# Router logits with three token blocks in each column group: shifted gate weights, two transposes, one copy and one bias product a batch

## The chip, the cores and the metric

One core of a Trainium2 chip runs the kernel. The metric is the device time of one execution in microseconds (us). Three runs of the kernel before gave 432.74, 435.83 and 438.20 us, so the median is 435.83 us.

## The reference

Two stages are computed, all in float32. The first is a chunked attention: 4 batches, 8 heads, 768 positions of width 64; a chunk of 32 queries sees 8 memory keys and a window of up to 56 keys around itself. Its output, as 3072 tokens of width 512, goes through a top-1 mixture of 8 experts. The change is in the router, the first lines of the second stage:

```python
logits = x @ w_gate + modality_bias[modality_id]      # (3072, 512) @ (512, 8)
e_idx = np.argmax(logits, axis=1)
probs = softmax(logits)
gate_w = probs[np.arange(N), e_idx]
for e in range(E):                                    # 8 experts, F = 1024
    h = np.maximum(x[mask] @ w1[e], 0.0)
    out[mask] = gate_w[mask, None] * (h @ w2[e])
```

## The kernel before

The order of the instructions is written out by hand for every engine (TensorE, VectorE, ScalarE, GpSimd, SyncE); an engine works through its own list in order.

**Attention.** There are 16 units `u`, two heads each, and each is done in two halves `hf`; the loop at L970 goes over the 32 halves `i` (and two more to drain). In a half TensorE makes scores (L328, 24 records: 12 products, each run twice for float32), transposes the scores (L345), makes the averages (L357) and transposes the result (L382); every second half it also transposes the next keys (L310, L314) or queries (L292). ScalarE takes most of it out of PSUM (L320, L297, L347, L385), VectorE subtracts the maximum and normalises (L336, L339, L365 to L370), GpSimd completes the windows of values (`share_v`, L271) and stores x (L375), SyncE issues the loads. Four PSUM banks named `tr` are handed out in turn by `bank()`.

**The routing of a batch.** Four units make one batch of 768 tokens, six blocks of 128. `xTs[u]` holds x transposed, with 128 features of unit u on the partitions and 768 tokens along the row, in one of five places of `xall`; the sixth place of `xall` is the buffer `lgs`. `route(b)` (L529) is a generator. First it makes the logits: for each half of the tokens, four products (L534), one for each unit g, write to the four column groups of one bank: 32 rows for each group, of which 8 are the experts' and 24 come from zero weights in `wg`. ScalarE copies each bank (384 columns) to `lgs` (L537). Later six transposes (L543), one for each block of 128 tokens, put tokens on the partitions, into two banks; two products (L526, `own_bias`) add the bias of each token's modality beside them; and two sums on VectorE (L548) add the four groups and the bias into `l`. Then come the maximum, the exponential, the ranks (L575 to L580) and the table of tokens by expert (L683).

**How the routing is woven in.** Each `yield "v"` ends a short VectorE step, each `yield "full"` waits for a place in TensorE's list. For batches 0 to 2 `pump` (L393) takes these steps out one by one at fixed places of the loop; the logits of batches 0, 1 and 2 go out at i = 10, 18 and 25 (the call `pump(1, ("tiled",))`, L1071), their transposes at i = 11, 19 and 26. Batch 3 is routed by `further` (L1132) between the first products of the experts.

**Experts.** The rest is matrix products of gathered tokens with float32 weights split into two parts (L844, L825, L828, L856), with VectorE and ScalarE making the parts (L755, L756). At the hand-over from attention to experts GpSimd gathers tokens (L765) and SyncE loads the first expert's weights (L748, L752).

GpSimd also makes the constants of the bias: `bias_rows` (L238 to L243) at i = 8. `small_loads` (L170) loads the gate weights at i = 1, and L928 zeroes `wg` at the start.

Of the kernel before, what the change touches and what calls it, by code (L numbers as in the profile page):

```python
# [9 lines left out]
F32 = mybir.dt.float32  # L10
# [7 lines left out]
AX = mybir.AxisListType  # L18
# [3 lines left out]
P = 128  # L22
B, H, S, D = 4, 8, 768, 64
NMEM = 8
NCH = S // 32
NT = S // P
E, DM, DF = 8, 512, 1024
# [18 lines left out]
def tile_chunk_attention_top1_moe(  # L46
# [14 lines left out]
    nc = tc.nc  # L61
# [4 lines left out]
    const = ctx.enter_context(tc.tile_pool(name="const", bufs=1))  # L66
    dram = ctx.enter_context(tc.tile_pool(name="dram", bufs=1, space=DRAM))
    ps = ctx.enter_context(tc.tile_pool(name="ps", bufs=2, space=PSUM))
    rt = ctx.enter_context(tc.tile_pool(name="rt", bufs=1))
# [5 lines left out]
    ld = c_ld.enter_context(tc.tile_pool(name="ld", bufs=3))  # L75
# [8 lines left out]
    def bank():  # L84
        return ps.tile([P, 512], F32, name="tr", tag="tr", bufs=4)
# [37 lines left out]
    ident = const.tile([P, P], F32, name="ident")  # L123
# [15 lines left out]
        nc.gpsimd.memset(mvx[g][:, :, D:D + 1], 1.0)  # L139
    edge_v(2)  # L140

    wg = const.tile([P, 4, 32], F32, name="wg")
    mod_i = ld.tile([N // P, P, 2], I32, name="mod_i", bufs=1)
    bias_b = ld.tile([N // P, 2, E], F32, name="bias_b", bufs=1)
    mods = const.tile([N // P + 1, P], F32, name="mods")
    rows_b = const.tile([N // P + 1, N // P, E], F32, name="rows_b")
# [21 lines left out]
                nc.vector.tensor_copy(vws[i][r, h, c, D:D + 1], vmask[r, m:m + 1])  # L168

    def small_loads():  # L170
        nc.sync.dma_start(wg[:, :, 0:E], w_gate.rearrange("(c p) e -> p c e", p=P))
        nc.sync.dma_start(mod_i.rearrange("t p w -> t (p w)"), modality.bitcast(I32).rearrange("(t x) -> t x", t=N // P))
        nc.sync.dma_start(bias_b, m_bias.rearrange("m e -> (m e)").partition_broadcast(N // P).rearrange("p (m e) -> p m e", e=E))
        nc.sync.dma_start(rows_b[N // P:], bass.AP(tensor=m_bias.tensor, offset=0, ap=[[0, 1], [0, N // P], [1, E]]))
# [28 lines left out]
    def more_constants():  # L203
        nc.vector.tensor_copy(iota5[:, :, 0:26], iota_i[:, 0:130].rearrange("p (a b) -> p a b", a=5))
        yield
        nc.vector.tensor_copy(iota3[:, :, 0:64], iota_i.rearrange("p (a b) -> p a b", a=3))
        yield
        nc.vector.tensor_scalar(rev[:, 0], iota3[:, 0, 0:E], -1.0, float(E), op0=ALU.mult, op1=ALU.add)
        yield
        nc.vector.memset(ones_b, 1.0)  # L210
        yield
        nc.vector.tensor_scalar(tri_b.rearrange("p (a b) -> p a b", a=2), iota3[:, 0:2, 0:64], pcol, None, op0=ALU.is_gt)
        yield

        nc.vector.tensor_scalar(tokn, iota3[:, 0, 0:N // P], float(P), pcol, op0=ALU.mult, op1=ALU.add)
        yield
        nc.vector.tensor_scalar(tokn, tokn, -EMPTY, None, op0=ALU.add)
        yield
        nc.vector.tensor_scalar(tokm, tokn, -1.0, None, op0=ALU.mult)
        yield  # L220
        nc.vector.memset(table, EMPTY)
        yield
        nc.vector.tensor_copy(tab_i[:, E * HI:NCOL], table[:, E * HI:NCOL])
        yield
        nc.vector.tensor_scalar(tail_row, pcol[0:64], 31.5, None, op0=ALU.is_gt)
        yield
        nc.vector.tensor_scalar(col0, iota3[0:64, 0, 0:E], float(HI), -float(E * HI), op0=ALU.mult, op1=ALU.add)
        yield
        nc.vector.memset(tot, 0.0)
        yield  # L230
        nc.vector.tensor_copy(four.rearrange("p (g t) -> p g t", g=4), ident[:, 0:REST].unsqueeze(1).to_broadcast([P, 4, REST]))
        yield
        nc.vector.tensor_scalar(quarter, pcol, 31.5, None, op0=ALU.is_gt)
        yield
        for r in (63.5, 95.5):
            nc.vector.scalar_tensor_tensor(quarter, pcol, r, quarter, op0=ALU.is_gt, op1=ALU.add)

    def bias_rows():  # L238
        nc.gpsimd.memset(mods, 1.0)
        nc.gpsimd.tensor_copy(mods[0:N // P], mod_i[:, :, 0])  # L240
        nc.gpsimd.tensor_sub(bias_b[:, 1:2], bias_b[:, 1:2], bias_b[:, 0:1])
        own = ident[0:N // P, 0:N // P].unsqueeze(2).to_broadcast([N // P, N // P, E])
        nc.gpsimd.tensor_mul(rows_b[0:N // P], bias_b[:, 1:2].to_broadcast([N // P, N // P, E]), own)  # L243


    qrs, qTs, xTs, xbs, PTs, kts, qts, scs, sbs, avs = ({} for _ in range(10))
# [130 lines left out]
    def trans_x(u, hf):  # L377
        xb = xbs[u]
        t = bank()
        warm(t, {(NU - 2, 0): 3, (NU - 2, 1): 2, (NU - 1, 0): 2}.get((u, hf), 0))  # L380
        for i in range(3):
            nc.tensor.transpose(t[:, i * P:(i + 1) * P], xb[:, 3 * hf + i, :], ident)  # L382
        if hf == 0:
            xTs[u] = xall[:, u % 5]
        nc.scalar.copy(xTs[u][:, 384 * hf:384 * hf + 384], t[:, 0:384])  # L385
        if hf == 1 and not NU - 3 <= u < NU - 1:
            store_x(u)


    xall = rt.tile([P, 6, S], F32, name="xall")  # L390
    routing, now = [], [0]

    def pump(k, pe=(), late=False):  # L393
# [128 lines left out]

    G = P + 32

    def own_bias(lt, T):
        nc.tensor.matmul(lt[:, 0:3 * G].rearrange("p (t c) -> p t c", c=G)[:, :, P:P + E], mods, rows_b[:, T:T + 3, :],  # L526
                         start=True, stop=True)

    def route(b):  # L529
        lgs = xall[:, 5]  # L530
        for hf in range(2):
            lg = bank()
            for g in range(4):
                nc.tensor.matmul(  # L534
                    lg[32 * g:32 * g + 32, 0:384], wg[:, g, :], xTs[4 * b + g][:, 384 * hf:384 * hf + 384], start=True, stop=True
                )
            nc.scalar.copy(lgs[:, 384 * hf:384 * hf + 384], lg[:, 0:384])  # L537
        yield "full"
        sh = [P, NT, E]
        l = sm.tile(sh, F32, name="l")  # L540
        lts = [bank() for _ in range(2)]
        for t in range(NT):
            nc.tensor.transpose(lts[t // 3][:, t % 3 * G:t % 3 * G + P], lgs[:, t * P:(t + 1) * P], ident)  # L543
        for i, lt in zip((0, 3), lts):
            own_bias(lt, b * NT + i)
        for i, lt in zip((0, 3), lts):
            parts = lt[:, 0:3 * G].rearrange("p (t g e) -> p t e g", t=3, g=5)[:, :, 0:E, :]
            nc.vector.reduce_sum(l[:, i:i + 3].unsqueeze(3), parts, axis=AX.X)  # L548
            yield "v"
        mx = sm.tile([P, NT, 1], F32, name="rmx")  # L550
        nc.vector.reduce_max(mx, l, axis=AX.X)
        yield "v"
# [95 lines left out]
        for t in range(NT):  # L648
# [8 lines left out]
            T = b * NT + t  # L657
# [267 lines left out]

    masks()
    nc.gpsimd.iota(iota_i, [[1, 192]], base=0, channel_multiplier=0)
    nc.gpsimd.memset(wg, 0.0)  # L928
    blank_v(0, 3)
    load_v(0)  # L930
    load_qk(1)
# [2 lines left out]
    t = ps.tile([P, 512], F32, name="av", tag="av", bufs=2)  # L934
# [28 lines left out]
    t = ps.tile([P, 512], F32, name="sc", tag="sc", bufs=2)  # L963
# [5 lines left out]
    n = len(units)  # L969
    for i in range(n + 2):  # L970
        live = i < n
        u, hf = units[i] if live else (NU, i % 2)
# [89 lines left out]
        for _ in range(4 if i > 2 else 0):  # L1062
            next(constants, None)
        if i == 8:
            bias_rows()
        if i == 5:
            nc.scalar.copy(mvx[1][:, :, 0:D], mvn[:, 1:2].to_broadcast([P, NCH, D]))
# [107 lines left out]

    tails = plan_tails()

    w1m = xall.rearrange("p a b -> p (a b)")[:, 0:4 * DF].rearrange("p (c f) -> p c f", c=4)

    def slot(s):  # L1180
        ahead = s != NSURE - 1
# [150 lines left out]
```

## Time and profile before

| | us |
|---|---|
| three runs, median | 435.83 (432.74 to 438.20) |
| the profiled execution | 436.68 |
| its span | 434.83 |
| outside the span | 1.85 |
| TensorE busy | 413.4 (95% of the span) |
| VectorE, ScalarE, GpSimd busy | 334.6, 299.4, 236.9 |

An engine's busy time is the union of its records; a product's end is modelled, so a busy TensorE need not be at its peak. The view by stretches tells how busy each engine is in one stage, the chain of waits tells which work ended last there, and the groups by line give the duration of one instruction.

### The profile page before, as it was taken

What the parts mean: (1) busy time and instruction counts of PE and PEld (TensorE: products, weight loads), DVE (VectorE), ACT (ScalarE), POOL (GpSimd) and SP (SyncE); (2) the same over time, 40 slices, a digit from 0 to 9 for tenths busy, and PEclk for the clock granted to TensorE, in tenths of its full rate; (3) what the DMA queues carried; (4) which work ended last, traced back from release to release, by engine and by line L of the source; (5) the groups of instructions that cost most, each with busy time, mean ns of one, the idle gap of its engine ahead of it and who ended that gap; (6) DMA issues with size and microseconds to landing.
All of it is one profiled execution on the core that took longest, in us unless ns stands there. A gap on an engine that the chain in (4) does not pass through costs nothing.

```text
span 434.8 us, 11397 instructions
## 1 busy us (share of the span) xinstructions
PE 413.4 (95%) x3867; PEld 343.5 (79%) x3870; DVE 334.6 (77%) x800; ACT 299.4 (69%) x597; POOL 236.9 (54%) x320
## 2 busy tenths in 40 slices
PE   7988999999996999999999999999999999999994
PEld 4776787778864878989898887888888788888882
DVE  6888589687774878957988888767988787978750
ACT  7776778687743564755767677767888786878750
POOL 8947768768583233877655564355577055620101
PEclk9999999999998999999999999999999999999998
DMA  9879999999759220117414629988977424220101
GB/s 220 177 196 223 253 255 202 252 226 227 150 145 328 97 51 0 52 49 148 97 50 98 233 90 274 236 269 237 293 270 239 102 54 100 69 79 2 49 3 54
DMA packets 82543, 66.81 MB, mean 154 GB/s; under 512 B 50659, under 2 KB 71339, under 8 KB 82476
## 3 DMA queue, kind: packets, MB, share of 16 engines
q1 hardware_dynamic: 75276, 46.36, 44.3%
q0 software_dynamic: 6784, 19.50, 14.3%
q8 instruction: 33, 0.54, 0.6%
q14 instruction: 34, 0.28, 0.2%
q10 hardware_dynamic: 416, 0.13, 0.1%
HBM read 84.64 MB, written 12.76 MB: 224 GB/s over the span
## 4 chain that ended last, share of the span: by engine, by line
PE 57%; issue 15%; DMA 10%; POOL 5%; DVE 5%; ACT 3%; another core or an unknown queue 1%; SPq 1%; POOLq 1%; ACTq 0%; DVEq 0%
PE tr L844 11%; PE sc L856 10%; PE av L856 9%; PE tr L825 7%; PE tr L828 4%; PE av L357 3%; DMA vw<-in_v_dram 3%; DMA out_dram<-o,ix_now 3%; DMA q<-in_q_dram 3%; PE sc L328 2%; ACT kbd L320 2%; POOL xg L765 2%; PE tr L382 2%; PE tr L345 2%; PE tr L310 1%
## 5 line engine op out<-in xcount | busy, mean ns | idle before, releaser
L756 DVE TENSOR_TENSOR w<-raw,w 128x512 fp32r<-128x512 f32 x96 | 67.3, 744 | 4.1 <-ACT w L755 3.2
L825 PE MATMUL tr<-xt,w 128*128 128x512 f32 x256 | 70.1, 395 | 0.0
L856 PE MATMUL av<-wh,h 128*128 128x512 f32 x192 | 62.7, 398 | 0.6 <-ACT wh L755 0.6
L271 POOL COPY vw<-vw 24x1472 f32<-24x1472 f32 x32 | 45.6, 1425 | 22.8 <-DMA vw<-in_v_dram 21.6
L755 ACT CAST w<-raw 128x512 fp32r<-128x512 f32 x96 | 53.8, 620 | 1.5 <-DMA raw<-in_moe_w_dram 1.5
L856 PE MATMUL sc<-wh,h 128*128 128x512 f32 x160 | 51.7, 397 | 0.0
L825 PEld LDWEIGHTS tr<-xt,w 128*128 128x128 f32 x256 | 44.3, 189 | 7.3 <-DVE h L838 0.4
L844 PE MATMUL tr<-xt,w 128*128 128x256 f32 x384 | 48.1, 284 | 0.7 <-DVE xt L820 0.7
L844 PEld LDWEIGHTS tr<-xt,w 128*128 128x128 f32 x384 | 46.8, 191 | 2.2 <-DVE xt L820 0.9
L320 ACT COPY kbd<-tr 64x672 f32<-64x672 f32 x57 | 44.5, 781 | 4.3 <-PE tr L314 2.8
L828 PEld LDWEIGHTS tr<-xt,w 128*128 128x128 f32 x256 | 39.3, 189 | 5.5
L856 PEld LDWEIGHTS av<-wh,h 128*128 128x128 f32 x192 | 36.1, 188 | 9.3 <-ACT wh L755 1.0
L861 POOL DMA_INDIRECT out_dram<-o,ix_now x22 | 25.8, 1173 | 29.9 <-ACT o L860 24.6
L828 PE MATMUL tr<-xt,w 128*128 128x256 f32 x256 | 40.7, 281 | 0.0
L834 DVE TENSOR_TENSOR hs<-tr,hs 128x256 f32<-128x256 f32 x64 | 26.8, 418 | 17.0 <-ACT hs L831 16.0
L856 PE MATMUL av<-wl,h 128*128 128x512 f32 x96 | 38.2, 397 | 0.4 <-DVE wl L756 0.2
L347 ACT ACTIVATE PT<-tr 128x384 f32<-128x384 f32 x32 | 15.8, 494 | 30.2 <-PE tr L345 24.6
L835 ACT ACTIVATE h<-hs 128x256 fp32r<-128x256 f32 x64 | 26.8, 419 | 13.9 <-DVE hs L834 12.6
L856 PEld LDWEIGHTS sc<-wh,h 128*128 128x128 f32 x160 | 30.1, 188 | 7.1 <-issue 0.2
L837 DVE TENSOR_TENSOR wl<-vw,wh 128x512 fp32r<-128x512 f32 x48 | 33.2, 692 | 2.1
L838 DVE SCALAR_TENSOR_TENSOR h<-hs,h 128x256 fp32r<-128x256 f32 x64 | 27.8, 434 | 7.8 <-ACT h L835 7.3
L831 ACT COPY hs<-tr 128x256 f32<-128x256 f32 x64 | 23.5, 368 | 13.8 <-PE tr L828 11.2
(265 smaller groups left out, 919.5 us busy)
## 6 DMA issues: line engine op xcount, KB each, us to landing
raw<-in_moe_w_dram SPq DMA_DIRECT2D x96, 256.0 KB
vw<-in_moe_w_dram SPq DMA_DIRECT2D x72, 256.0 KB
k<-in_k_dram SPq DMA_DIRECT2D x16, 384.0 KB
q<-in_q_dram SPq DMA_DIRECT2D x16, 384.0 KB
xd<-xb POOLq DMA_DIRECT2D x16, 384.0 KB
kbd<-in_moe_w_dram SPq DMA_DIRECT2D x24, 256.0 KB
vw<-in_v_dram SPq DMA_DIRECT2D x32, 184.0 KB
xall<-in_moe_w_dram SPq DMA_DIRECT2D x4, 1024.0 KB
```

Of the source, the lines that this page charges most:

```text
L271: nc.gpsimd.tensor_copy(vw[r0:r0 + 24, h, 1:NCH, 0:D], vw[r0 + 32:r0 + 56, h, 0:NCH - 1, 0:D])
L320: copy(dst.rearrange("p c (i j) -> p c i j", j=2)[:, :, :, j], win)
L755: nc.scalar.copy(wh[i], raw[i])
L756: (eng or nc.vector).tensor_sub(wl[i], raw[i], wh[i].bitcast(F32))
L825: nc.tensor.matmul(ph, wh[f][:, c * P:(c + 1) * P], xt[:, c].rearrange("p a n -> p (a n)"), start=(c == 0), stop=False, skip_group_check=True)
L828: nc.tensor.matmul(ph[:, 0:256], wl[f][:, c * P:(c + 1) * P], xth[:, c], start=False, stop=(c == 3), skip_group_check=True)
L834: nc.vector.tensor_add(hs, ph[:, 0:256], hs)
L835: nc.scalar.activation(hh[:, f], hs, AF.Relu)
L837: nc.vector.tensor_sub(wl[w], raw[w], wh[w].bitcast(F32))
L838: nc.vector.scalar_tensor_tensor(hl[:, f], hs, 0.0, hh[:, f].bitcast(F32), op0=ALU.max, op1=ALU.subtract)
L844: nc.tensor.matmul(ph, w[f][:, c * P:(c + 1) * P], x[:, c, :], start=(n == 0), stop=(n == 11))
L856: nc.tensor.matmul(pos[t], x, w[8 + f], start=(f == 0 and n == 0), stop=(f == 7 and n == 2))
```

## The change

The zeroed weights now come in three shifted copies. `wg3` has 120 columns for each unit: the 8 weights at columns 0, 40 and 80. A slice of 32 columns from 32k on thus has the weights in its columns 8k to 8k+7. The logits of a batch become twelve products of 256 columns into one bank: for k = 0, 1, 2 and each unit, the tokens of blocks k and 3+k (two runs of 128 columns) are multiplied with slice k and added up, so that the 32 rows of a column group hold three blocks of 8 logits. One copy of 256 columns, two transposes, one bias product of 48 columns and one sum over 48 results of five terms follow. One `yield "v"` falls away. GpSimd builds `wg3` at i = 8 (`gate_weights`), ahead of `bias_rows`; the zeroing of `wg` at the start falls away; `lgs` shrinks from 768 to 256 columns. The load of the gate weights stays where it was and now fills `wg` without gaps.

```diff
-    wg = const.tile([P, 4, 32], F32, name="wg")
+    wg = ld.tile([P, 4, E], F32, name="wg", bufs=1)
+    wg3 = const.tile([P, 4, 3 * 40], F32, name="wg3")
...
-        nc.sync.dma_start(wg[:, :, 0:E], w_gate.rearrange("(c p) e -> p c e", p=P))
+        nc.sync.dma_start(wg, w_gate.rearrange("(c p) e -> p c e", p=P))
...
+    def gate_weights():
+        nc.gpsimd.memset(wg3, 0.0)
+        nc.gpsimd.tensor_copy(wg3.rearrange("p c (q x) -> p c q x", x=40)[:, :, :, 0:E], wg.unsqueeze(2).to_broadcast([P, 4, 3, E]))
...
     def route(b):
-        lgs = xall[:, 5]
-        for hf in range(2):
-            lg = bank()
+        lgs = xall[:, 5 * S:5 * S + 2 * P]
+        lg = bank()
+        for k in range(3):
             for g in range(4):
                 nc.tensor.matmul(
-                    lg[32 * g:32 * g + 32, 0:384], wg[:, g, :], xTs[4 * b + g][:, 384 * hf:384 * hf + 384], start=True, stop=True
+                    lg[32 * g:32 * g + 32, 0:2 * P].rearrange("p (j n) -> p j n", j=2), wg3[:, g, 32 * k:32 * k + 32],
+                    xTs[4 * b + g].rearrange("p (j k n) -> p j k n", j=2, k=3)[:, :, k], start=(k == 0), stop=(k == 2),
+                    skip_group_check=True,
                 )
-            nc.scalar.copy(lgs[:, 384 * hf:384 * hf + 384], lg[:, 0:384])
+        nc.scalar.copy(lgs, lg[:, 0:2 * P])
         yield "full"
...
-        lts = [bank() for _ in range(2)]
-        for t in range(NT):
-            nc.tensor.transpose(lts[t // 3][:, t % 3 * G:t % 3 * G + P], lgs[:, t * P:(t + 1) * P], ident)
-        for i, lt in zip((0, 3), lts):
-            own_bias(lt, b * NT + i)
-        for i, lt in zip((0, 3), lts):
-            parts = lt[:, 0:3 * G].rearrange("p (t g e) -> p t e g", t=3, g=5)[:, :, 0:E, :]
-            nc.vector.reduce_sum(l[:, i:i + 3].unsqueeze(3), parts, axis=AX.X)
-            yield "v"
+        lt = bank()[:, 0:2 * G].rearrange("p (j c) -> p j c", j=2)
+        for j in range(2):
+            nc.tensor.transpose(lt[:, j, 0:P], lgs[:, j * P:(j + 1) * P], ident)
+        nc.tensor.matmul(lt[:, :, P:P + 3 * E], mods, rows_b[:, b * NT:(b + 1) * NT].rearrange("t (j k) e -> t j (k e)", j=2),
+                         start=True, stop=True)
+        parts = lt.rearrange("p j (g x) -> p j x g", x=32)[:, :, 0:3 * E, :]
+        nc.vector.reduce_sum(l.rearrange("p (j k) e -> p j (k e)", j=2).unsqueeze(3), parts, axis=AX.X)
+        yield "v"
...
-    nc.gpsimd.memset(wg, 0.0)
...
         if i == 8:
+            gate_weights()
             bias_rows()
```

## Rows read from the trace of the kernel before

**Rows 1.** The page's first part: busy time of each engine (share of span).

```profile
PE 413.4 (95%) x3867; PEld 343.5 (79%) x3870; DVE 334.6 (77%) x800; ACT 299.4 (69%) x597; POOL 236.9 (54%) x320
```

**Rows 2.** By stretches: from:to, length, busy PE PEld DVE ACT POOL, clock, DMA, GB/s.

```profile
40.00:70.00 30.00, 29.16 (x531) 23.39 (x529) 22.33 (x68) 23.38 (x43) 23.54 (x30) 1.00 1.02 235
70.00:112.00 42.00, 40.97 (x713) 33.84 (x715) 32.36 (x98) 31.29 (x58) 29.46 (x35) 1.00 1.03 236
112.00:140.00 28.00, 22.54 (x369) 16.81 (x363) 17.12 (x54) 14.77 (x30) 18.10 (x36) 0.94 0.69 196
140.00:195.00 55.00, 53.31 (x356) 46.05 (x352) 44.04 (x129) 31.57 (x67) 26.80 (x36) 1.00 0.19 58
195.00:425.00 230.00, 230.00 (x1367) 194.82 (x1366) 186.35 (x371) 169.34 (x359) 108.51 (x131) 1.00 0.52 141
```

**Rows 3.** Chain of waits around batch 0's routing: start, length, what.

```profile
57.13 3.43 DMA vw<-mvx
60.58 0.87 PE av L357 x24
```

**Rows 4.** Timeline of TensorE, batches 0 and 1: start, length, engine, line.

```profile
48.29 1.47 PE L534 MATMUL tr<-xall,wg 128*32 128x384 f32 x16
...
84.09 0.87 PE L357 MATMUL av<-vw,PT 128*32 128x130 f32 x24
...
84.78 0.84 PE L328 MATMUL sc<-kbd,qT 128*32 128x128 f32 x24
```

**Rows 5.** Chain of waits: batches 1, 2 and 3, and L903.

```profile
79.55 1.29 PE tr L534 x16
...
82.95 0.66 PE tr L543 x6
83.61 0.55 PE tr L526 x4
...
109.05 0.66 PE tr L543 x6
...
110.07 0.52 DVE l L548 x2
...
144.94 1.43 PE tr L534 x16
...
267.02 1.86 PE tr L903 x32
```

**Rows 6.** Groups by line and form, ScalarE, VectorE: busy us, mean ns | idle before.

```profile
L831 ACT COPY hs<-tr 128x256 f32<-128x256 f32 x64 | 23.5, 368 | 13.8 <-PE tr L828 11.2
L537 ACT COPY xall<-tr 128x384 f32<-128x384 f32 x8 | 3.7, 486 | 1.5 <-PE tr L534 1.5
L336 DVE TENSOR_REDUCE mx<-sc 128x6 f32<-128x384 f32 x32 | 17.4, 545 | 3.4 <-PE sc L328 3.4
L548 DVE TENSOR_REDUCE l<-tr 128x24 f32<-128x120 f32 x8 | 2.1, 278 | 3.1 <-PE tr L526 3.1
```

**Rows 7.** Timeline of ScalarE at batch 2's logits.

```profile
107.32 0.48 ACT L537 COPY xall<-tr 128x384 f32<-128x384 f32 x1 [1.17 <-PE tr L534]
...
107.99 0.48 ACT L537 COPY xall<-tr 128x384 f32<-128x384 f32 x1 [0.19 <-PE tr L534]
...
109.15 0.49 ACT L347 ACTIVATE PT<-tr 128x384 f32<-128x384 f32 x1 [0.68 <-PE tr L345]
```

**Rows 8.** Groups by line and form, GpSimd.

```profile
L302 POOL COPY kbd<-memT 64x192 f32<-64x192 f32 x28 | 9.7, 347 | 5.1 <-PE sc L328 3.7
L127 POOL MEMSET vw<- 128x256 f32 x3 | 0.9, 314 | 0.0
L928 POOL MEMSET wg<- 128x128 f32 x1 | 0.2, 204 | 0.0
```

**Rows 9.** Timeline of GpSimd behind the bias constants.

```profile
46.95 1.40 POOL L271 COPY vw<-vw 24x1472 f32<-24x1472 f32 x1 [0.74 <-DMA vw<-in_v_dram]
```

**Rows 10.** Chain of waits at the hand-over to the experts.

```profile
127.74 5.48 another core or an unknown queue
```

More of the change, by code (lines that the diff above doesn't have):

```diff
@@ L383, in trans_x @@
         if hf == 0:
-            xTs[u] = xall[:, u % 5]
+            xTs[u] = xall[:, u % 5 * S:(u % 5 + 1) * S]
         nc.scalar.copy(xTs[u][:, 384 * hf:384 * hf + 384], t[:, 0:384])
@@ L387, in trans_x @@
             store_x(u)
-    xall = rt.tile([P, 6, S], F32, name="xall")
+    xall = rt.tile([P, 5 * S + 2 * P], F32, name="xall")
     routing, now = [], [0]
@@ L523, in tile_chunk_attention_top1_moe @@
     G = P + 32
-    def own_bias(lt, T):
-        nc.tensor.matmul(lt[:, 0:3 * G].rearrange("p (t c) -> p t c", c=G)[:, :, P:P + E], mods, rows_b[:, T:T + 3, :],
-                         start=True, stop=True)
     def route(b):
-        lgs = xall[:, 5]
-        for hf in range(2):
-            lg = bank()
+        lgs = xall[:, 5 * S:5 * S + 2 * P]
+        lg = bank()
+        for k in range(3):
             for g in range(4):
                 nc.tensor.matmul(
-                    lg[32 * g:32 * g + 32, 0:384], wg[:, g, :], xTs[4 * b + g][:, 384 * hf:384 * hf + 384], start=True, stop=True
+                    lg[32 * g:32 * g + 32, 0:2 * P].rearrange("p (j n) -> p j n", j=2), wg3[:, g, 32 * k:32 * k + 32],
+                    xTs[4 * b + g].rearrange("p (j k n) -> p j k n", j=2, k=3)[:, :, k], start=(k == 0), stop=(k == 2),
+                    skip_group_check=True,
                 )
-            nc.scalar.copy(lgs[:, 384 * hf:384 * hf + 384], lg[:, 0:384])
+        nc.scalar.copy(lgs, lg[:, 0:2 * P])
         yield "full"
@@ L1176, in tile_chunk_attention_top1_moe @@
     tails = plan_tails()
-    w1m = xall.rearrange("p a b -> p (a b)")[:, 0:4 * DF].rearrange("p (c f) -> p c f", c=4)
+    w1m = xall[:, 0:4 * DF].rearrange("p (c f) -> p c f", c=4)
     def slot(s):
```

## The prediction

> **What bounds the kernel now.** I read the page's busy times first: TensorE is busy for 413.4 of 434.8 us and no other engine comes near [rows 1]. Then the stretches [rows 2], since a share over the whole says little about one place. TensorE is busy for 97 to 98% of the time from 40 to 112 us, where the first three batches are routed, and for 97% from 140 to 195, where the fourth is; from 195 to 425 it never stops. Only from 112 to 140, the hand-over to the experts, does it idle: 5.5 us of 28, and it is the only one of these stretches in which the granted clock is below full (0.94: for part of it at the lower level, 1.2 GHz). One thing disturbs this picture: from 40 to 112 the DMA share is 1.02 to 1.03, so the transfers are as full as TensorE. Hence the third view, the chain of waits: which of the two ended last where the routing stands?
>
> For batch 0 it is the transfers. The chain runs through the transfer of the memory rows until 60.56, and the averages (L357) start at 60.58 [rows 3]; batch 0's logits start at 48.29 [rows 4], and the chain does not pass through them. For batches 1, 2 and 3 it runs through the router's products themselves [rows 5]. So a shorter routing on TensorE should shorten the kernel there, one for one.
>
> **The change part by part, for one batch.**
>
> *Logits.* Eight products of 384 columns become twelve of 256, which is 3072 columns either way. Four column groups run together, so the 16 records of before are four sets in 1.29 us, 0.32 us each [rows 5]. L903 has the same form with 256 columns: 32 records, eight sets, 1.86 us, so 0.23 us a set and 1.40 us for six. That is the upper end, +0.11 us, since L903's piece also carries its way into and out of full-width products. The lower end is the same rate by column: 0. What each product reads comes in two runs of 128 columns now. L357 already reads two runs (of 65), and it starts 0.69 us ahead of L328, six sets of 130 columns [rows 4]: 0.115 us a set and 0.88 ns a column, against 1.29 us / (4 x 384) = 0.84 ns for one run. So two runs cost hardly anything. I take +0.05.
>
> *Transposes.* Six take 0.66 us, 0.11 each [rows 5]; four go: -0.44.
>
> *Bias.* Four records take 0.55 us, 0.14 each [rows 5]. A transpose makes 128 columns in 0.11 us, so 24 columns are about 0.02 us: the price is by record, not by column. Two records of 48 columns then take 0.275 us: -0.275. If the price went by column, nothing would be saved; that is the other end.
>
> TensorE so gets 0.44 + 0.275 - 0.05 = 0.66 us a batch, between 0.33 (bias unchanged, logits +0.11) and 0.72.
>
> *Copy.* Two copies of 384 columns at 486 ns become one of 256; L831 has that form at 368 ns [rows 6]. ScalarE gains 2 x 0.486 - 0.368 = 0.60 us of work a batch. I count it at nothing: TensorE's transposes and averages cover it, and the chain of batches 1 and 3 does not pass through these copies. Without that cover it would be a gain.
>
> The one thing that could speak against it is that one bank now has to be complete before any copy starts. At batch 2 the two copies start at 107.32 and 107.99, and the second ends at 108.47 [rows 7]. The new one starts with the second's start and ends at 107.99 + 0.37 = 108.36, so it is ready sooner; ScalarE waits some 0.67 us longer ahead of it, and its next work, the exponential at 109.15, waited 0.68 us for TensorE anyway. The Trainium skill (Perfetto Trace Analysis, section Matmuls) says to let independent groups go through different banks, so that emptying one overlaps the next one's products, and that larger products are the more efficient. By the first rule the lost overlap could cost up to 0.67 us a batch and bring the sum back to no change; by the rows it is covered, the smaller copy makes up for it, and the sum stays as below. It is a rival.
>
> *Sum on VectorE.* 120 elements take 278 ns, 384 take 545 [rows 6]: 1.01 ns an element, so 240 take 0.40 us, and 0.16 us of 0.56 is saved. It counts only at batch 2, where the chain leaves TensorE into these sums (0.52 us from 110.07 [rows 5]): -0.12.
>
> *Steps.* One `yield "v"` less moves every later VectorE step of batches 0 and 1 one place up in the lists; followed through the loop, the rank products (i = 13 and 21) and the table products (i = 16 and 24) stay where they are. The exponential of the logits moves ahead of the key copies on ScalarE; its input is made one half `i` earlier, so nothing queued behind it waits for more than its own short run, which ScalarE spends anyway. Price: nothing. A batch also takes two `tr` banks fewer, so a product waits for an older bank than before, never for a newer one.
>
> *GpSimd.* Zeroing 128 columns takes 204 ns, 256 take 314 [rows 8]: 0.86 ns a column, so 480 take 0.51 us. The copy writes 96 elements a partition; a copy of 192 takes 347 ns [rows 8], an upper end. Together 0.7 to 0.86 us, ahead of `share_v` at 46.95, which waited 0.74 us for its load [rows 9]. So it is covered, up to 0.12 us late; were the cover gone, `share_v` and the averages that need it would come 0.86 us later. The 204 ns zeroing at the start goes: a gain of at most 0.20 us, counted as nothing.
>
> **The sum.** Batch 0: 0, since the transfers end last there (other end -0.66). Batch 1: -0.66. Batch 2: transposes, logits and the sums' end: -0.44 + 0.05; from the transposes' end (109.05 + 0.66 = 109.71) the chain took 0.36 us to the sums and 0.52 for them [rows 5], now 0.28 + 0.02 and 0.40: -0.18; together -0.57. Batch 3, inside the experts' products, where TensorE is 97% busy: -0.66. In all -1.9 us on 436.68 us, the profiled execution (434.83 span, 1.85 around it): 434.8. That execution is 0.85 us above the median, so against the median I forecast 433.9 us.
>
> **The rivals.**
>
> *The hand-over takes it back.* At 127.74 us the chain has 5.48 us that no engine in the profile ends [rows 10], as much as TensorE idles in this stretch [rows 2]. If the end of that stop is set by transfers (the stretch's first weights and gathers), then what batches 1 and 2 gained before it is waited for there, and only batch 3's 0.66 us stays: 436.0 in the profile's terms, 435.2 against the median. For it: DMA is the fullest resource until 112 us. Against: the first expert is named by batch 2's ranks, so its loads are issued earlier too, and the DMA share of the stretch is only 0.69 [rows 2].
>
> *The stop is shorter or gone.* It is a single event, and the three runs differ by 5.5 us, about its size. Without it: 433.9 - 5.5 = 428.4. Nothing in the change aims at it; only the moment moves by 1.2 us.
>
> *The stop is longer: slower.* The same place. The gain of 1.9 us is used up once it lasts longer than 5.48 + 1.9 = 7.4 us. A second stop of its size would give 433.9 + 5.5 = 439.4; half of that, 436.6.
>
> *ScalarE holds it up.* One bank, no overlap: if in each batch the 0.67 us longer wait for the logits stood in front of work that TensorE needs, the 0.66 us of each batch would be gone: 435.8, no change. Against: the exponential behind the copy waits for TensorE anyway [rows 7].
>
> *The change does not do what it says:* sets of 256 columns cost what sets of 384 do, 0.32 us. Six are 1.93 us, +0.64, and batches 1 to 3 gain nothing: 435.8. L903's 0.23 speaks against it.
>
> **How the numbers follow.** Forecast 0.52; the hand-over takes it back 0.20; stop shorter or gone 0.10; stop longer 0.12; ScalarE 0.04; sets too dear 0.02. The predicted time is the forecast's, 433.9; its own range is 433.2 (batch 0 gains too) to 434.9 (the bias saves nothing). The range for 8 in 10 reaches from 431.0 (half of the stop gone) to 436.6 (half a stop more). About 2%, 8.7 us, is what a measurement of this kernel can tell from no change: faster than 427.1 needs more than the whole stop to go, 0.03; slower than 444.5 needs a stop over 16 us, 0.03; within it 0.94.
>
> **What would show it.** Right: L534 with 24 records in about 1.3 us, L543 with two in 0.22, L526 with two in 0.28; from the logits of batch 1 to those of batch 2 some 0.7 us less; the start of the long unbroken products near 195 about 1.9 us earlier. Wrong: `share_v` after i = 8 later and a wait of the averages for it; the chain through transfers at batch 1 too; a stop at 127 that ends when it did before.

## The result and the profile after

The changed kernel takes 433.4 us (median) where the kernel before took 436.38 beside it: a ratio of 0.9909 (95% interval 0.9884 to 0.9934), some 3 to 5 us. The ratio is that of the fast runs' means and leaves out five of the changed kernel's 22 runs, those over 1.5% above its fastest (427.80 us), and none of the kernel before; the two medians alone give 0.9932. Measured twice more, on two chips, the ratio is 0.9944 (0.9919 to 0.9969) and 0.9947 (0.9915 to 0.9979). Taken together that is about 0.993, 3 us. The 433.4 us lie in the range of the prediction, beside its 433.9; but the forecast's 1.9 us are a ratio of 0.9957, which the first interval excludes and the other two, whose middles lie below it, do not. So the direction and TensorE's share of the mechanism were right and the size was too small, while the first pair of profiles (436.68 and 431.75 us) shows more than the change does.

The page's busy times, and the stretches of [rows 2], in the changed kernel:

```profile
PE 410.7 (96%) x3878; PEld 342.5 (80%) x3878; DVE 335.6 (78%) x796; ACT 298.0 (69%) x593; POOL 236.5 (55%) x321
...
40.00:70.00 30.00, 29.16 (x541) 24.04 (x540) 23.53 (x69) 23.94 (x44) 23.65 (x32) 1.00 1.05 238
70.00:112.00 42.00, 40.72 (x752) 33.90 (x751) 33.55 (x99) 32.28 (x59) 30.42 (x37) 1.00 1.01 235
112.00:140.00 28.00, 23.38 (x347) 18.47 (x347) 18.14 (x55) 13.32 (x28) 17.18 (x36) 0.94 0.75 223
140.00:195.00 55.00, 53.95 (x369) 47.17 (x368) 44.03 (x124) 32.08 (x68) 29.48 (x40) 1.00 0.19 56
195.00:425.00 230.00, 228.44 (x1338) 192.23 (x1337) 183.62 (x367) 167.35 (x354) 104.28 (x128) 1.00 0.52 138
```

Nothing changes its kind: TensorE is still the engine that is busy throughout, the transfers are still full until 112 us, and the stretch from 112 to 140 still has 4.6 us in which TensorE idles. VectorE is busier in the first two stretches (23.53 against 22.33 us, 33.55 against 32.36), though it has less to do; that will matter below.

The routing in the chain of waits of the changed kernel (start, length, what), batches 0, 1, 2 and 3, against [rows 4, 5]:

```profile
48.27 1.29 PE tr L535 x24
...
51.69 0.22 PE tr L546 x2
51.91 0.35 PE tr L547 x2
...
77.71 1.30 PE tr L535 x24
...
103.83 1.38 PE tr L535 x24
...
141.44 1.43 PE tr L535 x24
```

All four batches are in the chain now, batch 0 too. The logits cost what they did (24 records in 1.29 us, before 16 in 1.29), the transposes 0.22 for 0.66, the bias 0.35 for 0.55. TensorE's own saving is therefore 0.44 + 0.20 - 0.00 = 0.64 us a batch; the sum had 0.66.

### The profile page after: what moved, and what is told of

Same layout as the page of the kernel before. It is cut to its first block, busy times and chain, and to the rows that moved or that the text cites. A ratio compares the mean times of both kernels' runs of the same rounds, so it can differ in the third digit from the quotient of the medians.

```text
span 429.9 us, 11405 instructions
## 1 busy us (share of the span) xinstructions
PE 410.7 (96%) x3878; PEld 342.5 (80%) x3878; DVE 335.6 (78%) x796; ACT 298.0 (69%) x593; POOL 236.5 (55%) x321
## 4 chain that ended last, share of the span: by engine, by line
PE 40%; issue 21%; POOL 12%; DMA 12%; DVE 8%; ACT 4%; POOLq 1%; SPq 0%; DVEq 0%; ACTq 0%
PE tr L846 10%; DMA out_dram<-o,ix_now 7%; PE av L858 7%; POOL xg L767 6%; PE sc L858 5%; PE av L362 4%; ACT kbd L325 3%; DMA vw<-in_v_dram 2%; PE sc L333 2%; PE tr L387 2%; POOL planes L792 2%; PE tr L827 2%; PE tr L350 2%; PE tr L297 2%; POOL out_dram L863 1%
## 5 line engine op out<-in xcount | busy, mean ns | idle before, releaser
L758 DVE TENSOR_TENSOR w<-raw,w 128x512 fp32r<-128x512 f32 x96 | 64.4, 715 | 4.1 <-ACT w L757 3.6
```

Of the source, the lines that this page charges most:

```text
L758: (eng or nc.vector).tensor_sub(wl[i], raw[i], wh[i].bitcast(F32))
```

## Where each piece of time went, over all traces

The starts of the averages (L357 before, L362 after) cut the span into pieces of one half `i` each. The logits of batches 0, 1 and 2 lie between halves 9 and 10, 17 and 18, 24 and 25; the hand-over between 29 and 31; batch 3 behind 31. All lengths in us, worked out from the traces; the experiments in the lower part are told below. Four pieces without routing (10-11, 12-13, 18-19, 20-21) are 3.27 us long in every trace, to 0.01, so a piece is a fine measure of what happens in it.

| trace | 9-10 | 17-18 | 24-25 | 9 to 25 | 29-31 | 31 to end |
|---|---|---|---|---|---|---|
| before | 5.71 | 5.41 | 6.24 | 64.07 | 11.34 | 295.59 |
| e0_before | 5.71 | 5.71 | 6.58 | 63.94 | 5.78 | 294.24 |
| e6_gate_weights | 5.74 | 5.71 | 5.92 | 63.31 | 11.16 | 295.58 |
| f3_before_gates_late | 5.72 | 5.70 | 5.92 | 63.54 | 7.35 | 294.47 |
| *mean, old routing* | 5.72 | 5.63 | 6.17 | 63.72 | | 294.97 |
| after | 4.79 | 4.78 | 5.37 | 60.93 | 11.08 | 294.13 |
| e0_after | 5.19 | 4.78 | 5.39 | 61.72 | 5.78 | 293.74 |
| f1_after | 5.09 | 4.78 | 5.36 | 63.36 | 12.29 | 294.08 |
| e5_gates_late | 4.78 | 4.78 | 5.36 | 62.08 | 7.07 | 294.77 |
| f4_loads_first | 4.78 | 4.78 | 5.37 | 62.59 | 8.81 | 294.24 |
| *mean, new routing* | 4.93 | 4.78 | 5.37 | 62.14 | | 294.19 |
| e1_pe_back | 5.44 | 5.44 | 5.94 | 64.60 | 5.78 | 294.22 |
| e2_pe_twice | 6.32 | 6.32 | 6.90 | 66.40 | 5.79 | 295.09 |
| e3_act_dve_back | 5.23 | 5.23 | 6.76 | 63.21 | 11.91 | 295.62 |
| f2_act_only | 5.25 | 4.95 | 6.51 | 63.34 | 11.04 | 294.10 |
| e4_banks_back | 5.51 | 5.48 | 5.64 | 63.39 | 11.13 | 294.21 |

Three things stand in it. In the pieces with the routing the change saves 0.79, 0.85 and 0.80 us in the mean, together 2.44. From half 9 to 25 only 1.58 of this is left: 0.86 is given back in pieces without routing. And behind half 31 it saves 0.78.

The means hold events of single executions, and the pieces without them say more. For batches 0 and 1 they are 5.71 before and 4.78 after (in e0_after and f1_after TensorE stops within batch 0's logits, 0.4 and 0.3 us); that is 0.93. For batch 2 they are 5.92 and 5.37, which is 0.55: in the two old traces with 6.24 and 6.58 the records of averages and logits stand mixed up there, and one of them has a stop besides. The next piece (25-26) takes 0.17 of it back, 4.30 for 4.13 in the mean; why was not taken apart. For batch 3, from the start of half 31's averages to the end of its bias products, it takes 11.32 to 11.33 us in all four old traces and 10.68 to 10.70 in all five new ones, 0.64 less. What the mean behind half 31 has beyond that comes some 18 us later: in before, e6_gate_weights and e5_gates_late TensorE waits there 0.4 to 0.6 us for weights that ScalarE converts (L755 before).

## The experiments

The runs stand in three blocks, each on a chip of its own, beside the same runs of the kernel before (428.76, 436.49 and 436.70 us).

| kernel | us | ratio to before | 95% interval |
|---|---|---|---|
| e0_before (one run) | 428.42 | | |
| e0_after | 426.46 | 0.9944 | 0.9919 to 0.9969 |
| e1_pe_back | 429.21 | 1.0009 | 0.9982 to 1.0036 |
| e2_pe_twice | 432.85 | 1.0105 | 1.0073 to 1.0136 |
| e3_act_dve_back | 435.08 | 0.9967 | 0.9947 to 0.9987 |
| e4_banks_back | 433.84 | 0.9951 | 0.9932 to 0.9969 |
| e5_gates_late | 428.94 | 0.9829 | 0.9798 to 0.9859 |
| e6_gate_weights | 436.24 | 0.9986 | 0.9969 to 1.0003 |
| f1_after | 433.76 | 0.9947 | 0.9915 to 0.9979 |
| f2_act_only | 434.43 | 0.9928 | 0.9898 to 0.9958 |
| f3_before_gates_late | 432.41 | 0.9907 | 0.9874 to 0.9939 |
| f4_loads_first | 430.53 | 0.9858 | 0.9831 to 0.9885 |

### Both kernels again: e0_before, e0_after

> The kernel before once more, for a second trace. Theory (TensorE's own time): every step between the two kernels that the routing makes is there again with this trace: the averages behind batch 0's logits start some 0.9 us earlier in the changed kernel, batch 3's part is some 1.5 us shorter. Rival (one execution's luck): the idle 0.50 us ahead of the keys' transposes at 77.91, which only the trace of before has, and batch 3's part beyond 0.66 us are single events and are missing here, so that the two traces lie 0.7 to 1.5 us nearer to one another than 4.9 us.

> The changed kernel once more, timed. Theory: the ratio to the kernel before stays at 0.991 (0.988 to 0.994), some 4 us, twice the 1.9 us of the forecast. Rival (the forecast was right and the rest was luck): 0.9955, that is 1.9 us.

The steps that the routing makes are there again: 0.52, 0.93 and 1.19 us, where the first pair has 0.92, 0.63 and 0.87. The idle 0.50 us ahead of 77.91 and batch 3's surplus are missing here, as the rival had it: behind half 31 the second pair differs by 0.50 us (294.24 and 293.74), the first by 1.46. The surplus is no single event, though: e6_gate_weights has it too (295.58). The ratio falls between the two expectations. f1_after, the changed kernel a third time, was expected at 0.991 if the stop at the hand-over showed; it shows, and the ratio is 0.9947, so the first pair's 0.9909 did not come again. What e0_before settles is batch 0. Its chain of waits, in the place where that of [rows 3] had a transfer from 57.13 to 60.56:

```profile
47.16 1.29 PE tr L534 x16
...
50.72 0.80 PE tr L543 x6
51.52 0.55 PE tr L526 x4
52.07 0.80 PE av L357 x24
```

The same program, and here the chain runs through batch 0's logits, transposes and bias. In the first trace the transfer ended 0.02 us ahead of the averages at 60.58, and TensorE's own last product ahead of them 0.03 us (timeline of TensorE):

```profile
60.37 0.18 PE L580 MATMUL tr<-oh,tri_b 128*128 128x48 bf16 x1
```

The transfer had won a tie, and the tie was no evidence that TensorE had time to spare.

### TensorE's work put back: e1_pe_back, e2_pe_twice

```diff
         for j in range(2):
             nc.tensor.transpose(lt[:, j, 0:P], lgs[:, j * P:(j + 1) * P], ident)
+        for j in range(4):      # 10 in e2_pe_twice
+            nc.tensor.transpose(ltb[:, 2 * G:2 * G + P], lgs[:, j % 2 * P:(j % 2 + 1) * P], ident)
...
+        for j in range(1):      # 2 in e2_pe_twice
+            nc.tensor.matmul(ltb[:, 2 * G + P:2 * G + P + 6 * E].rearrange("p (j c) -> p j c", j=2), mods,
+                             rows_b[:, b * NT:(b + 1) * NT].rearrange("t (j k) e -> t j (k e)", j=2), start=True, stop=True)
```

> The changed kernel with TensorE's work put back: in each batch four more transposes and a second bias product (two records) into columns of the same bank that nobody reads. That is 4 x 0.11 + 2 x 0.14 = 0.72 us a batch; ScalarE, VectorE, the banks and the steps stay as changed. Theory (TensorE's own time counts in all four batches): 4 x 0.72 = 2.9 us of the 4 come back, the ratio is 0.9975, and the averages behind batch 0 start only about 0.2 us earlier than in the kernel before. Rival 1 (in batch 0 the transfers end last, as forecast): the averages behind batch 0 stay where the changed kernel has them, 2.2 us come back, the ratio is 0.996. Rival 2 (what ScalarE and VectorE were relieved of makes the gain): nothing comes back, 0.991.

> The same with ten more transposes and two more bias products (four records) a batch: 10 x 0.11 + 4 x 0.14 = 1.65 us a batch. Theory: 4 x 1.65 = 6.6 us on the changed kernel, 2.6 us slower than before: 1.006. Rival (hidden beside transfers, ScalarE or VectorE up to some point): less than half of that, 0.998 or lower.

The chain of e2_pe_twice at batch 0 (L547 are the two real transposes, L549 the added ones, L550 the two real bias records, L553 the four added ones):

```profile
51.28 0.22 PE tr L547 x2
51.50 1.09 PE tr L549 x10
52.59 0.35 PE tr L550 x2
52.94 0.45 PE tr L553 x4
```

By such rows e1_pe_back adds 0.44 + 0.22 = 0.66 us a batch (a bias product behind another takes 0.22, only the first takes 0.35) and e2_pe_twice 1.09 + 0.45 = 1.54. On the changed kernel they cost 429.21 - 426.46 = 2.75 and 432.85 - 426.46 = 6.39 us, against 4 x 0.66 = 2.64 and 4 x 1.54 = 6.16. One us of TensorE's work in the routing is one us of the kernel, in all four batches: the pieces with batches 0 and 1 grow by 0.66 and 1.54 against the undisturbed 4.78, the piece with batch 2 by 0.57 and 1.53, batch 3's stretch by 0.65 and 1.53. That decides for the theory, against the forecast's zero for batch 0, and against relief of ScalarE as the main carrier: with TensorE's work back, the kernel is as slow as before (1.0009). In batches 0 and 1 the piece of e1_pe_back stays 0.27 us below that of the old routing (5.44 and 5.71), in batch 2 it does not (5.94 and 5.92). These 0.27 us are not TensorE's own time; the next part shows what they are.

### Relief of ScalarE and VectorE, banks, GpSimd: e3, f2, e4, e6

```diff
         nc.scalar.copy(lgs, lg[:, 0:2 * P])
+        nc.scalar.copy(lgs, lg[:, 0:2 * P])                # e3_act_dve_back
+        nc.scalar.copy(lgs[:, 0:P], lg[:, 0:P])            # e3_act_dve_back
+        nc.scalar.copy(spare, lgs)                         # f2_act_only
+        nc.scalar.copy(spare[:, 0:P], lgs[:, 0:P])         # f2_act_only
...
         nc.vector.reduce_sum(l.rearrange("p (j k) e -> p j (k e)", j=2).unsqueeze(3), parts, axis=AX.X)
+        nc.vector.reduce_sum(l[:, 0:1].unsqueeze(3), parts[:, 0, 0:E].unsqueeze(1), axis=AX.X)      # e3_act_dve_back
```

> The changed kernel with the work of ScalarE and VectorE put back: behind each batch's logits copy a second one of 256 columns and one of 128 (ScalarE then has 2 x 0.37 + 0.24 = 0.98 us a batch where the kernel before has 0.97), behind the sum a further small one (about 0.2 us). TensorE's part stays as changed. Theory (only TensorE's time counts): 0 to +0.5 us on the changed kernel, the ratio to the kernel before is 0.9945 to 0.996, where the changed kernel had 0.9944. Rival (the relief of ScalarE and VectorE carries the gain, TensorE's part being only one of two that end together): 4 x 0.6 = 2.4 us come back, 1.000.

> The changed kernel with ScalarE's 0.6 us a batch put back as pure load: behind the logits copy two copies from that copy's result in SBUF (256 and 128 columns) into a tile that nothing reads. No bank is held longer, and the transposes do not wait for them. Theory 1 (what e3_act_dve_back lost hangs on the longer way from the logits to the transposes, not on ScalarE's time): steps of 4.8, 4.8 and 5.4 us, 0 to 0.5 us on the changed kernel. Theory 2 (ScalarE's time itself is close behind TensorE's): 5.2 us in batches 0 and 1 as in e3_act_dve_back, 1.3 to 2.4 us on the changed kernel.

Pure load on ScalarE (f2_act_only) has a lower ratio than the changed kernel beside it (0.9928 and 0.9947) and a higher median (434.43 and 433.76 us): in the time of a run nothing can be told apart. The ratio of e3_act_dve_back, 0.9967, is above the others, but its interval overlaps that of the changed kernel; a loss of up to 1 us is possible and not shown. The pieces show more. With ScalarE's load back those of batches 0 and 1 are 5.25 and 4.95 us, where the changed kernel has 4.78 undisturbed, and 5.23 in both in e3_act_dve_back, where the transposes wait for the second copy and the bank is held longer. So f2_act_only meets neither theory: the steps are not those of theory 1, the time is not that of theory 2. TensorE's transposes of batch 0's logits wait in it for ScalarE (start, length; in brackets idle before and releaser):

```profile
51.19 0.44 PE L549 MATMUL tr<-ident,xall 128*128 128x128 f32 x2 [0.25 <-ACT PT L352]
```

The same wait stands in the kernel before. ScalarE and TensorE in e0_before at batch 0, as in seven of the eight old pieces with batches 0 and 1:

```profile
49.25 0.87 ACT L537 COPY xall<-tr 128x384 f32<-128x384 f32 x2
49.99 0.52 ACT L347 ACTIVATE PT<-tr 128x384 f32<-128x384 f32 x1
...
50.17 0.55 PE L382 MATMUL tr<-ident,xb 128*128 128x128 f32 x3
50.57 0.95 PE L543 MATMUL tr<-ident,xall 128*128 128x128 f32 x6
```

and in the eighth, before at batch 1 (5.41 us):

```profile
82.07 0.49 ACT L347 ACTIVATE PT<-tr 128x384 f32<-128x384 f32 x1 [0.34 <-PE tr L345]
...
82.79 0.82 PE L543 MATMUL tr<-ident,xall 128*128 128x128 f32 x6
```

In e0_before ScalarE goes from one bank to the next without a pause, and TensorE's groups start 0.05 to 0.06 us after it is through with one (50.12 and 50.17, 50.51 and 50.57): the six transposes take 0.95 us. In the eighth piece TensorE had stopped for 0.50 us shortly before, at 77.41; ScalarE has caught up and waits for TensorE, and the six take 0.82. The difference over the whole piece, 5.71 against 5.41, is 0.30 us. In the changed kernel the groups have the short form in every piece with batches 0 and 1. So of the 0.93 us that the change saves in each of these two batches 0.64 are TensorE's own work, and the other 0.3 are waits for ScalarE that its relief takes away. How they divide between the shorter copy and the two banks fewer was not taken apart. e3_act_dve_back and f2_act_only have a long piece at batch 2 because TensorE stops there for 1.0 us; that is told at the end.

```diff
         nc.scalar.copy(lgs, lg[:, 0:2 * P])
+        for _ in range(2):
+            nc.tensor.matmul(bank()[:, 0:2], idle[:, 0:P], idle[:, P:P + 2], start=True, stop=True)
```

> The changed kernel with two more banks taken in each batch, behind the logits copy, each for a product of two columns (some 0.03 us each by the shortest records of the trace): the rotation of the four banks is that of the kernel before. Theory: nothing but the products themselves, 0 to +0.3 us, ratio 0.9945 to 0.995. Rival (older banks are what lets TensorE run ahead): 0.5 to 1 us a batch comes back, 0.999 or more.

The ratio, 0.9951, is at the theory's end and not to be told from the changed kernel's 0.9944 and 0.9947. But the pieces of batches 0 and 1 are 0.73 and 0.70 us longer than 4.78, which is the rival's price; the time of the run does not show it. TensorE's timeline in it, second of the two small products:

```profile
48.25 0.16 PE L542 MATMUL tr<-idle 128*128 128x2 bf16 x1 [0.32 <-ACT kbd L325]
```

It waits 0.32 us until ScalarE has emptied the bank with the keys. The kernel before took two banks for the logits and two for the transposes, at two places; this one takes three at one place, so it is harsher than the rotation of the kernel before, against its expectation, and it does not tell how much of the 0.3 us hangs on banks. That a bank taken costs a wait where ScalarE is busy is shown.

```diff
+    def gate_weights():      # in the kernel before
+        nc.gpsimd.memset(wg3, 0.0)
+        nc.gpsimd.tensor_copy(wg3.rearrange("p c (q x) -> p c q x", x=40)[:, :, :, 0:E], wg[:, :, 0:E].unsqueeze(2).to_broadcast([P, 4, 3, E]))
...
+            gate_weights()
             bias_rows()
```

> The kernel before with GpSimd's new work alone: the zeroing of 480 columns and the copy of the gate weights into a tile that nothing reads, ahead of the bias rows (503 + 263 = 0.77 us). Theory (covered by a wait for the value rows): 1.000, and the averages of halves 9 to 12 start no later than in the traces of the kernel before. Rival: the shared value rows come 0.77 us later and the averages with them, 1.002.

0.9986 with 1 inside the interval, and the pieces from half 9 to 12 are 5.74, 3.27 and 3.93 us (old routing elsewhere: 5.71 to 5.72, 3.27, 3.91 to 4.00). GpSimd's part costs nothing that can be seen. In the changed kernel it takes 0.77 us, inside the forecast 0.7 to 0.86 (groups by line and form: busy us, mean ns):

```profile
L240 POOL MEMSET wg<- 128x480 f32 x1 | 0.5, 503 | 0.1
L241 POOL COPY wg<-wg 128x96 f32<-128x96 f32 x1 | 0.3, 263 | 0.1
```

### The stop at the hand-over: e5, f3, f4

```diff
             conv(0)
             other = second()
-            fetch(gd[0:N - S], slice(DM, XW))
             for f in range(8, 16):
                 nc.gpsimd.memset(raw[f][0:1, 0:1], 0.0)
             load_w(0, 1)
+            fetch(gd[0:N - S], slice(DM, XW))     # f4_loads_first
...
+    fetch(gd[0:N - S], slice(DM, XW))             # e5_gates_late, f3_before_gates_late
     keep(0)
```

> The changed kernel with the two gathers of the first expert's gates moved from the last half of the loop to just ahead of the copy that needs them, so that GpSimd has two indirect transfers instead of four there. Theory A (where the stop of 7 us between the averages of halves 29 and 30 shows, it lasts until GpSimd's fourth gather is through): halves 29 to 30 take 4.5 us or less there, 2 us and more faster than the changed kernel. Theory B (the stop belongs to the chip on which it is run and has nothing to do with the gathers): the same as the changed kernel, within 0.3 us of 2.46 where it does not show and of 6.6 where it does; the ratio to before is that of the changed kernel.

> The kernel before with the two gathers of the gates moved as in e5_gates_late. Theory (the stop lasts until GpSimd's last gather is through; the routing and the stop are separate): where the stop shows, 0.9917, that is 3.6 us faster than the kernel before, and the step between halves 29 and 30 is 4.3 us or less; where it does not, 1.000. Rival (the gain of e5_gates_late came from elsewhere in the changed kernel): 1.000 with the stop in place.

> The changed kernel with all four gathers in place, but GpSimd's small zeroings and the weight loads that wait for them ahead of the last two gathers instead of behind: the loads start as early as in e5_gates_late. Theory A (the gathers make the stop): the step between halves 29 and 30 stays above 6 us where the changed kernel has it. Rival (the later weight loads make it): it falls to 3.7 us as in e5_gates_late.

The stop of [rows 10] shows in the first pair and on two of the three chips of the experiments, in both kernels alike; on the chip of the first block it never does (29 to 31 takes 5.78 to 5.79 us in all four traces there). GpSimd and VectorE in f1_after, which has it (start, length; in brackets idle before and releaser):

```profile
126.09 0.96 POOL L767 DMA_INDIRECT xg<-xd,gx  x1 [0.31 <-issue]
127.05 0.18 POOL L1103 MEMSET raw<- 1x1 f32 x4
127.40 0.94 POOL L767 DMA_INDIRECT xg<-gd,gx  x1 [0.17 <-issue]
128.65 0.94 POOL L767 DMA_INDIRECT xg<-gd,gx  x1 [0.30 <-issue]
...
130.57 0.17 DVE L370 TENSOR_SCALAR den<-av 128x6 f32<-128x6 f32 x1 [5.25 <-remote]
```

and in e0_after, which does not:

```profile
125.62 0.95 POOL L767 DMA_INDIRECT xg<-gd,gx  x1 [0.17 <-issue]
126.88 0.94 POOL L767 DMA_INDIRECT xg<-gd,gx  x1 [0.31 <-issue]
...
127.15 0.17 DVE L370 TENSOR_SCALAR den<-av 128x6 f32<-128x6 f32 x1 [0.42 <-PE av L362]
```

The gathers are the same to 0.01 us. In e0_after VectorE goes on while they run; in f1_after it hears from TensorE only 0.98 us after the last of them has ended (129.59), though the averages that it waits for were over at 126.4. In e5_gates_late:

```profile
124.56 0.96 POOL L767 DMA_INDIRECT xg<-xd,gx  x1 [0.31 <-issue]
...
126.23 0.16 DVE L370 TENSOR_SCALAR den<-av 128x6 f32<-128x6 f32 x1 [2.39 <-PE tr L350]
```

With two gathers the wait is 2.39 us and ends 0.71 us after the second: theory A, on a chip that has the stop (halves 29 to 30 take 3.74 us, in f3_before_gates_late 4.02). By its ratio the kernel is the fastest of all, 0.9829, and the same edit in the kernel before is worth 0.9907, so it is a matter of its own (0.9907 x 0.993 = 0.984). f4_loads_first agrees with neither expectation:

```profile
126.04 0.96 POOL L767 DMA_INDIRECT xg<-xd,gx  x1 [0.31 <-issue]
...
127.74 0.94 POOL L767 DMA_INDIRECT xg<-gd,gx  x1 [0.34 <-issue]
128.99 0.95 POOL L767 DMA_INDIRECT xg<-gd,gx  x1 [0.30 <-issue]
...
127.69 0.17 DVE L370 TENSOR_SCALAR den<-av 128x6 f32<-128x6 f32 x1 [2.43 <-PE tr L350]
...
131.21 0.17 DVE L370 TENSOR_SCALAR den<-av 128x6 f32<-128x6 f32 x1 [1.48 <-PE av L362]
```

Its four gathers leave a gap of 0.74 us between the second and the third, where f1_after leaves 0.35. VectorE hears from TensorE in that gap, 0.69 us after the second gather, and again 1.27 us after the fourth: one stop became two, and 29 to 31 takes 8.81 us instead of 11.0 to 12.3. So on these chips the wait follows GpSimd's gathers, run by run, with the loads moved and with them in place. What in a gather holds TensorE's signals back, and why one chip is free of it, none of these runs shows.

## Why the prediction was right, and where its steps failed

*The terms of TensorE* were right, together 0.64 us a batch for 0.66: logits 0.00 (forecast +0.05, bounds 0 and 0.11), transposes -0.44, bias -0.20 (forecast -0.275, bounds 0 and -0.275). The price of the bias is by record, but the first product behind the transposes has 0.13 us on top, which the four records of [rows 5] spread out.

*Batch 0: 0* failed. The step was "the transfers end last there". The other end of the term, -0.66, was the true one for TensorE's work: one for one in e1_pe_back and e2_pe_twice, and with ScalarE's part the piece is 0.93 us shorter. The chain of [rows 3] named the transfer because it ended last, 0.02 us ahead of the averages; that says which of two ended last in this execution, not how far the other was ahead of it. e0_before shows it the other way round.

*"Copy. I count it at nothing"* failed in batches 0 and 1, by 0.3 us each. The reason given, that TensorE's work covers it and the chain of batches 1 and 3 does not pass through the copies, was read from the one old piece of eight in which ScalarE had caught up.

*Batch 1: -0.66, batch 2: -0.57, batch 3: -0.66* were right for TensorE's work: 0.64 less in batch 1 (in before itself 5.41 to 4.78) and in batch 3, 0.55 in batch 2, of which the next piece gives 0.17 back. What the means show above that is ScalarE's 0.3 in batch 1 and single executions' events in batches 2 and 3. Batch 2's shorter way through VectorE is not shown: TensorE's groups alone make the 0.55 there (transposes -0.44, bias -0.20, and the scores behind the logits 0.85 for 0.77).

*"Steps. Price: nothing"* failed in part, and this takes some 0.5 of the 0.86 us that are given back. VectorE in f1_after behind batch 0, GpSimd and TensorE beside it:

```profile
52.35 2.88 POOL L276 COPY vw<-vw 24x1472 f32<-24x1472 f32 x2 [2.66 <-DMA vw<-in_v_dram]
...
52.50 0.19 DVE L553 TENSOR_REDUCE rmx<-l 128x6 f32<-128x48 f32 x1
52.73 1.09 DVE L555 TENSOR_TENSOR l<-l,rmx 128x48 f32<-128x48 f32 x1
53.85 1.43 DVE L559 SCALAR_TENSOR_TENSOR eq<-l,rev 128x48 f32<-128x48 f32 x1
...
56.72 0.52 PE L350 MATMUL tr<-ident,sb 128*128 128x128 f32 x3 [1.26 <-DVE c L568]
```

and in e0_after:

```profile
52.88 0.21 DVE L555 TENSOR_TENSOR l<-l,rmx 128x48 f32<-128x48 f32 x1
53.13 0.21 DVE L559 SCALAR_TENSOR_TENSOR eq<-l,rev 128x48 f32<-128x48 f32 x1
```

The same two instructions on 48 elements take 0.42 us or 2.52, and the second ends (55.28) when GpSimd's two copies do (55.23). The one with a single input tensor (L553) is not held. The Trainium skill (SBUF — State Buffer, section "SBUF: two separate sides") says that a VectorE operation with two SBUF inputs and a GpSimd operation that reads SBUF take a shared pair of ports as an exclusive lock, and that the loser fully blocks; the trace agrees, 1.09 and 1.43 us against 0.21. Behind these two waits the softmax of the next half (its last step stands just ahead of `c`), so TensorE waits 1.26 us, and the piece from half 11 to 12 is 4.95 us long instead of 3.94. GpSimd's copies start when a transfer lands, so the meeting is a matter of each execution, but not an even one: `eq` of batch 0 or 1 takes 1.38 to 1.44 us in six of the ten traces with the new routing and in none of the four with the old, which has 0.32 at most. In three of these four the copy meets the step before it (the subtraction, L555 above, of batch 0, 0.49 to 0.94 us), and the piece 11-12 is no more than 0.09 us longer for it. The routing's steps come 0.8 us and one place earlier; that this makes them meet the copies more often fits, and no run tested it. The pieces 11-12 and 19-20 take 0.32 and 0.19 us more in the mean over the five traces; the rest of the 0.86 is the piece 16-17 (+0.38), told in the last section.

*GpSimd: nothing* held (e6_gate_weights). VectorE's 0.16 us was not measured by itself.

*The rivals.* "The hand-over takes it back" falls: 29 to 31 takes no longer after the change where two traces stand beside one another (11.08 for 11.34, 5.78 for 5.78), so the stop moved with the work. "ScalarE holds it up" falls, and the rows above show the opposite: ScalarE held the kernel before up. "Sets of 256 cost what sets of 384 do" falls by 24 records in 1.29 us. "The stop is shorter or gone" was a matter of the chip: where it does not show, both kernels are 7 to 8 us faster and the change is worth the same. The argument for this rival, that the three runs' spread of 5.5 us is the stop's size, is not borne out: on a chip every trace with the gathers in their place has the stop, or none. Some runs without a trace lie as far below the rest (427.80 us in the first pair, 431.20 of the kernel before in the third block), so a single execution without it is not excluded.

*What would show it:* the records came as said (24 in 1.29, two in 0.22, two in 0.35 for 0.28); from the logits of batch 1 to those of batch 2 it takes 26.13 us for 26.88, 0.75 less. The long products start 4.97 us earlier, not 1.9: 0.20 ahead of half 9, 3.14 from 9 to 25 (1.58 in the mean over the traces), 0.15 from 25 to 31 and 1.48 behind 31 (0.84 in the mean). The surplus over the means is this one pair's luck: the stop at 77.41 of the kernel before, told in the last section, the mixed records at its batch 2 and the wait for ScalarE behind its batch 3.

*The number.* That 433.9 stands so near 433.4 is in part luck. The forecast left out some 1.2 us that the change saves (batch 0's 0.64 and ScalarE's 0.3 in two batches) and some 0.7 us that go elsewhere (the meetings with GpSimd, the piece behind batch 2), and the kernel before was measured 0.55 us higher beside it than in the three runs. Two ends of its ranges are not exact: a bias that saves nothing gives about 434.6 by the same rows, not 434.9, and half of the stop gone 431.15, not 431.0.

## What to carry to other kernels

Where a chain of waits shows a transfer that ends 0.02 us ahead of the compute, count both as binding: put the compute's work back, or twice of it, and see whether the time follows one for one, as it did here (2.75 and 6.39 us for 2.64 and 6.16). The same holds for cover: a copy that one execution covers can be one that is waited for in all the others (here in seven pieces of eight, 0.3 us each), so a second trace of the kernel before is worth taking ahead of the sum. Work that comes earlier meets other work: a small VectorE step with two SBUF inputs can stand for as long as a GpSimd copy beside it, so a moved step has a price there even when its own time is the same. And one execution's stop should be looked for on another chip before it is put into a sum; here a stop of 5 us that had nothing to do with the change could be shortened on its own, by moving two gathers out of it (0.9907 in the kernel before).

## What the runs showed of the hardware that was not expected

On two of the three chips of the experiments TensorE's signals stay out while GpSimd's indirect gathers follow one another within 0.35 us, and come 0.7 to 1.3 us after the last; on the third chip the same instructions hold nobody.

TensorE stops between products with no other engine that it waits for. In f2_act_only, in half 24:

```profile
103.48 0.43 PE L362 MATMUL av<-vw,PT 128*32 128x130 f32 x8
104.93 0.65 PE L362 MATMUL av<-vw,PT 128*32 128x130 f32 x16 [1.02 <-issue]
```

The traces have a DMA queue named instruction (queue and kind: packets, MB, share; kernel before):

```profile
q8 instruction: 33, 0.54, 0.6%
```

It brings blocks of 16 KB during the execution, one every 4 to 11 us here, most of them without any stop. The stops of this kind of over 0.25 us between 70 and 107 us, nine in eight kernels, all end 1.3 to 1.6 us after such a block has arrived, and the smaller and earlier ones, down to 0.10 us and to 40 us, 1.3 to 1.7 us after one. The block ahead of the stop shown came at 103.5, in the kernel before it came at 76.4 (TensorE, idle from 77.41, goes on at 77.91), in f1_after, e5_gates_late and f4_loads_first at 74.9, 73.8 and 73.9 (it goes on at 76.19, 75.12 and 75.33). They make the long pieces at batch 2 in f2_act_only and e3_act_dve_back, and three of the five changed traces have one in the piece 16-17, which is 0.38 us longer in the mean than with the old routing, where one of four has it. That TensorE then waits for its own instructions, brought late by the full transfers, fits all nine; whose instructions the blocks hold is not shown, and no run tested it.
